# A linear-attention and gated-FFN kernel: the first batch in smaller pieces, with a new order of the whole program

## The chip, the core and the metric

The kernel runs on one core of a Trainium2 chip. The metric is the device time of one execution in microseconds (us); before the change the median of three runs is 379.01 us (378.92 to 380.15).

## What is computed

```python
def _attn_ref(q, k, v, w_phi):              # q, k, v: 8 batches, 8 heads, 576 tokens, 64
    def phi(x):
        proj = np.einsum('bhsd,df->bhsf', x, w_phi)              # 64 -> 128 features
        proj = proj - np.max(np.abs(proj), axis=-1, keepdims=True)
        return np.concatenate([np.exp(proj), np.exp(-proj)], axis=-1)
    q_p, k_p = (phi(q), phi(k))
    kv = np.einsum('bhsf,bhsd->bhfd', k_p, v)
    z = np.sum(k_p, axis=2)
    num = np.einsum('bhsf,bhfd->bhsd', q_p, kv)
    den = np.einsum('bhsf,bhf->bhs', q_p, z)[..., None] + 1e-06
    return num / den

def _moe_ref(x, w_gate, w_val, w_out):      # x: 4608 tokens, 512; 1536 inner columns
    gate = np.maximum(x @ w_gate, 0.0)
    val = x @ w_val
    return gate * val @ w_out
```

The attention's result of all heads is the FFN's x. Inputs and output are float32; the kernel multiplies in bf16.

## The kernel before, in words

**Tiling.** Each batch has 512 main tokens, in four chunks of 128, and a tail of 64; tails of two batches are worked together (`u`, `km`, `vm`, `qm`), and all tails make the FFN's ninth group. For batches 0 and 1 (`b < TURN`), keys are taken in pairs of heads, 36 blocks in all, cut by `K_CUTS` into five or six items per batch, and K and Q are transposed on TensorE; later batches use DMA transposes.

**Steps of a batch.** Each step is an *atom*: a small function with a key, made in the order of the code. For keys: `kT` transposes, `kTc` copies the transpose out of PSUM, `kr` multiplies by `w_phi` (64 rows of the array; two heads side by side on the two halves, `par` 0 and 1), `km` takes the maxima of the absolute values (DVE), `ke` the two exponentials (ACT), `kk` the scales, `vs` scales v by them (POOL, or DVE if the order's number has a prime), `kv` multiplies, `kvc` copies the result out. For queries: `qT`, `qTc`, `qc` (features by columns, for the exponentials `qe`), `qr` (features by rows, for the maxima `qm`), `qk` (the scale `cq`), `n` the numerators of three, three and two heads, `nt` and `nu` their sums on DVE, `xu` the division (a reciprocal on DVE, a product on POOL), then the transpose into x: `xT` and `xc` on TensorE for batches 0 and 1, `xd` by DMA after that.

**FFN.** Group g has 12 inner column blocks f: `fv` is the value half and `fg` the gate half (four matmuls each into a PSUM bank; the value half is copied to `val_sb` by ACT or DVE, the gate half is multiplied with it on DVE into `h`), `fo` the output matmuls in thirds, followed for the last third by a copy and the store. Group 0 is cut into steps by `FIRST`, entries of (first chunk, last chunk, first f, last f); the last tile of the ninth group is cut into columns by `LAST`.

**Order.** `ORDER`, a text of numbers, says in which order the atoms are written out; a prime chooses the other engine for a copy or a product; `z3` are three matmuls on zeros. Each engine runs its instructions in that order and waits on semaphores for what it reads and for buffers to come free. DMAs are issued by SP (loads in float32, transposes, stores), by ACT (halves of the last stores) and by POOL (loads that convert to bf16: q, k, the thirds of `wv` and `wg`, and `wo`); each issues them in its place among its other instructions. The first loads, of `w_phi`, k and v of batch 0, stand ahead of the order and are not changed. PSUM has eight banks, given out by `bank()`.

Of the kernel before, what the change touches and what calls it, by code (L numbers as in the profile page):

```python
# [8 lines left out]
FP32 = mybir.dt.float32  # L9
# [7 lines left out]

K_CUTS = [[4, 8, 16, 24, 32], [8, 16, 24, 32]]

FIRST = ((0, 2, 0, 4), (2, 4, 0, 4), (0, 4, 4, 12))  # L20
# [3 lines left out]


ORDER = """7 z3 82 92 93 83' 84 87 94 86 8 0 98 102 85 89 90 91 88 103 z1 104 96 97 108 105 95 107 106 z1 112
113 109 99 101 110' 111 122 114 115 123' 124 127 118 116 132 1 117 133 119 120 121 125 100' 128 z1
148 149 129 126 187 10 134 188 151 153 155 137 2 131 156 135 158 160 142 130 196 144 136 200 198
150 154 236 139 141 237 143 140 246 247 157 159 152 29 161 162 226 190 192 54 138 256 257 175 163
194 176 164 165 189 145 147' 191 266 177 146 3 267 193 4 169 170 166 167 171 168 195 199 181 178  # L30
182 321 214 5 172 179 183 180 184 201 197 217 215 11 220 221 218 222 219 208 9 322' 216 173 174'
282 283 223 209 185 186' 202 203 238 227' 210 205 206 204 207 240 211 1092 1093 1094 224 225' 239
1095 1096 324 328 228 229 242 212 213' 1097 326 232 1098 1099 1100 1101 1102' 231 6 1103 1104 1105
1106 1107 230 241 1108 243 268 269 270 271 273 258 274 272 261 248 251 260 249 253 255 254 1109 252
259 263 39 1110' 1111 1112' 264 1113 1114 275 250 233 1115 1116' 1117 290 361 262 363 265 292 365
279 280' 281' 323 327 291 295 293 1118 1119 294 1120' 1121 284 325 288 330 30 51 332 334 234 245
244 235 276 277 329 333 285 287 13 40 278' 289 1122 1123 351 296 1124 335 352 353 309 312 310 311
# [3 lines left out]
347' 32 55 61 371 372 307 308' 16 1134 63 388 398 402 399 391 400 383 385 1135' 1136 389 1137 401  # L41
42 403 1138' 405 393 367 368 369 395 392 394 390 1139 1140 1141 33 1142' 1143 1144' 17 43 424 426
428 384 418 454 458 420 1145 456 1146' 422 1147 1148 460 462 464 465 419 421 423 508 512 509 1149
# [4 lines left out]
502 1163 1164 1165' 534 536 538 564 529 531 523 1166 1167 568 503 570 476 574 566 533 569 571 1168  # L48
573 515 514 516 572 18 1169 1170 535 517 539 528 537 530 488 491 524 492 525 526 527 532 1171' 1172
1173 1174 1175 489 563 66 67 565 20 45 504 34 505 506 69 19 44 1176 1177 493 36 1178' 495 1179 567  # L50
507' 1180' 1181 494 490 590 555 496 497 1182' 593 575 591 68 587 588 589 540 1183 592 594 541 542
# [3 lines left out]
585 586 643 1199 1200 46 72 657 661 659 646 650 647 616 619 1201' 608 648 618 649 651 652 609 1202  # L55
# [3 lines left out]
675 676 716 717 741 1217 672 673 677 718 719 704 705 706 707 708 709 47 1218' 1219 1220 1221 1222  # L59
669 670 721 722 723 671 1223 1224 674 720 724 740 615 1225 1226 683 684 685 756 757 725 746 747 749  # L60
53 766 770 768 678 679 743 759 1227 1228 750 1229 1230' 710 711 712 760 713 758 761 763 714 680 681
# [4 lines left out]
1250' 1251 25 74 78 784 77 836 840 838 75 79 76 1252' 1253 831 832 1254 1255 1256' 1257 833 1258  # L66
814 846 847 848 1259 1260 785 786 828 829 830 787 48 834 835 815 817 818 1261 1262' 1263 800 1264
779 780 819 820 821 822 816 823 24 1265 37 1266 1267 1268 864 865 781 788 789 80 884 885 888 867
854 856 824 1269 1270' 866 1271 1272 887 858 889 868 855 857 849 1273 1274 891 850 851 869 859 900
904 902 874 877 28 894 896 1275 1276' 876 875 879 881 1277 1278 1279' 871 1280' 1281 843 878 886  # L70
880 898 844 845 852 1282 1283 81 895 899 901 903 929 933 1284 931 897 1285 905 1286 1287 964 870
853 930 934 968 890 965 935 937 966 1288' 1289 939 932 967 882 883 1290 872 873 974 978 976 861 936
# [4 lines left out]
1308 962 963 1309' 1310 1010 990 1008 1005 1040 1007 1012 57 1044 1006 1014 1009 991 1311 1042 1312  # L77
1313 1314 1051 1011 1000 1013 1045 1047 1049 1039 992 993' 1015 982 1315' 1043 1041 1316' 1001 1002
1003' 1317 1318' 1319 1320 1321 1322' 1323 1324' 971 972 1325 1016 973' 1023 983 1031 1055 1056
1326' 1024 1052 1327 1057 1025 1053 1054 1328' 1329 1034 1035 1330 1058 1059 1060 1061 1063 1064  # L80
1065 1331 1332 1333 1020 1036 1334' 1032 1033 1017 1018 1019 1021 1022 1062 1069 1335 1026 1027
1336 1337 1338 1028 1029 1030 1066 1067 1068 1339 1340 1070 1071 1037 1038 1074 1078 1075 1079 1072
1073 1077 1341 1342 1343 1344 1345' 1346 1347 1348' 1349 1350 1351' 1352' 1353 1354 1355 1356' 1357
1358' 1076 1080 1087 1359 1084 1085 1088 1089 1360 1361 1362 1363 1364' 1365 1366' 1367 1368' 1369
1086 1081 1082 1083 1090 1370 1371 1372 1091 1373 1374 1375 1376 1377 1378 1379 1380 1381' 1382
1383 1384' 1385 1386 1387' 1388 1389 1390' 1391 1392 1393 1394' 1395 1396 1397 1398' 1399 1400 1401
1402' 1403 1404' 1405 1406 1407 1408' 1409 1410' 1411 1412 1413 1414' 1415 1416 1417 1418 1419
1420' 1421 1422 1423 1424 1425 1426'"""
# [31 lines left out]
def kernel(  # L120
# [120 lines left out]
    def load_val_gate(t, w, i):  # L241
# [4 lines left out]
        )  # L246

    for i in range(NS):
        atoms.add("ld", f"wv{i}")(lambda alt, i=i: load_val_gate(wv_sb, moe_w_val, i))
        atoms.add("ld", f"wg{i}")(lambda alt, i=i: load_val_gate(wg_sb, moe_w_gate, i))  # L250
    atoms.add("ld", "wo")(
        lambda alt: nc.gpsimd.dma_start(
            out=wo_sb, in_=moe_w_out.rearrange("(c p) n -> p c n", p=P)
        )
    )
    for b in range(B):
        if b:
            atoms.add("ld", f"k{b}")(lambda alt, b=b: load_k(b))
# [23 lines left out]
    def turned_copy(st, n, by):  # L282
        st["T"] = sb_T.tile([P, n, P], BF16, name=f"tT{n}", bufs=3 if n == 4 else 2)
        copy_by(by)(st["T"].rearrange("p a b -> p (a b)"), st["pt"][:, 0 : n * P])

    for b in range(TURN, B):
        for n in "kq":

            @atoms.add("turn", n, b)
# [574 lines left out]
```

## Time and profile before

| | |
|---|---|
| median of three runs | 379.01 us (378.92 to 380.15) |
| profiled execution: its span | 377.4 us |
| median less that span, outside the program's instructions | 1.6 us |
| PE (TensorE) busy | 368.1 us, 98% |
| DVE (VectorE) busy | 290.7 us, 77% |
| ACT (ScalarE) busy | 213.1 us, 56% |
| POOL (GpSimd) busy | 151.3 us, 40% |
| moved by DMA | 45.10 MB, mean 120 GB/s |

The profile is of one execution; of its time only the span is given, from the first instruction of the program to the last. A share over the whole span hides stages: the rows by stage in the prediction are the ones to read. Matmuls overlap in the records, so a busy PE may still lose a little between two of them. An entry such as `L734` is a line of the kernel before; the functions above carry these numbers.

### The profile page before, as it was taken

The page shows a single profiled execution, that of the slowest core. Times are in us where ns is not written, and L with a number is a line of the kernel's source. Part 1 is how long each engine was busy: PE and PEld are TensorE (multiplying, and loading weights), DVE is VectorE, ACT ScalarE, POOL GpSimd, SP SyncE. Part 2 cuts the span into 40 slices and gives each one's busy share as a digit, 9 for nine tenths or more (in the row PEclk, how much of TensorE's full clock was granted, in tenths as well). Part 3 has the DMA queues.
Part 4 walks back from the last instruction along what each step waited for, and adds up shares of the span by engine and source line. Part 5 has one row for each costly group of instructions (what it writes and reads, how often), then busy time and mean ns, then how long its engine had stood idle before and what let it go on. Part 6 is the DMA issues. An engine that isn't in the chain of part 4 may idle for free.

```text
span 377.4 us, 8960 instructions
## 1 busy us (share of the span) xinstructions
PE 368.1 (98%) x3502; PEld 197.4 (52%) x3502; DVE 290.7 (77%) x633; ACT 213.1 (56%) x509; POOL 151.3 (40%) x201
## 2 busy tenths in 40 slices
PE   7789999999999999999999999999999999999996
PEld 4568465546545555464554554465455444444443
DVE  6998999988876799888868886988768927824641
ACT  6997888877687556876765359882740302111101
POOL 5883672488275275901842126933700210000000
PEclk9899999999999999999999999999999999999999
DMA  8999999999489959781289678620410130021004
GB/s 260 205 200 215 233 131 174 219 172 137 89 213 236 165 67 171 144 182 28 59 160 179 96 174 132 130 16 16 128 41 2 29 113 29 2 67 58 2 2 109
DMA packets 87929, 45.10 MB, mean 120 GB/s; under 512 B 55824, under 2 KB 82000, under 8 KB 87888
## 3 DMA queue, kind: packets, MB, share of 16 engines
q1 hardware_dynamic: 60208, 30.42, 37.3%
q0 software_dynamic: 27200, 13.57, 28.8%
q8 instruction: 27, 0.44, 0.5%
q10 hardware_dynamic: 480, 0.56, 0.5%
q14 instruction: 14, 0.11, 0.1%
HBM read 37.78 MB, written 9.44 MB: 125 GB/s over the span
## 4 chain that ended last, share of the span: by engine, by line
PE 92%; ACT 3%; DMA 3%; issue 0%; SPq 0%; DVE 0%; POOL 0%; DVEq 0%
PE pa L734 49%; PE pa L791 25%; PE pa L597 5%; PE pa L312 5%; PE pa L486 4%; PE pa L549 2%; DMA qn<-in_q_dram 2%; ACT qp L567 2%; PE pa L271 1%; PE pa L509 1%; DMA vn<-in_k_dram 1%; ACT kp L368 1%; ACT kv L422 0%; ACT val_sb L749 0%; ACT xT L662 0%
## 5 line engine op out<-in xcount | busy, mean ns | idle before, releaser
L791 PE MATMUL pa<-wo_sb,h 128*128 128x512 bf16 (+2 forms) x444 | 99.9, 373 | 0.0
L734 PE MATMUL pa<-xT,wv_sb 128*128 128x512 bf16 (+1 forms) x400 | 99.3, 370 | 0.1
L734 PE MATMUL pa<-xT,wg_sb 128*128 128x512 bf16 (+1 forms) x400 | 99.3, 370 | 0.0
L756 DVE SCALAR_TENSOR_TENSOR h<-pa,val_sb 128x512 bf16<-128x512 f32 (+1 forms) x112 | 74.6, 669 | 27.2 <-PE pa L734 20.5
L749 ACT CAST val_sb<-pa 128x512 bf16<-128x512 f32 (+1 forms) x67 | 38.1, 575 | 97.1 <-PE pa L734 88.0
L567 ACT ACTIVATE qp<-pa 128x512 bf16<-128x512 f32 x144 | 76.2, 618 | 15.1 <-PE pa L549 14.8
L368 ACT ACTIVATE kp<-pa 128x512 bf16<-128x512 f32 (+1 forms) x152 | 77.4, 605 | 11.1 <-PE pa L312 9.8
L328 POOL TENSOR_TENSOR vs<-vn,ek 128x512 bf16<-128x512 f32 (+1 forms) x68 | 67.4, 1005 | 31.1 <-DMA vn<-in_v_dram 15.2
L734 PEld LDWEIGHTS <-wv_sb 128*128 128x128 bf16 x448 | 41.9, 98 | 44.9 <-issue 1.2
L734 PEld LDWEIGHTS <-wg_sb 128*128 128x128 bf16 x448 | 41.6, 98 | 43.5 <-issue 0.7
L791 PEld LDWEIGHTS <-h 128*128 128x128 bf16 x444 | 40.8, 98 | 44.6 <-issue 0.8
L319 DVE TENSOR_REDUCE mq<-pa 128x4 f32<-128x512 f32 x72 | 46.5, 683 | 10.4 <-PE pa L312 10.1
L319 DVE TENSOR_REDUCE mk<-pa 128x4 f32<-128x512 f32 (+1 forms) x76 | 47.8, 653 | 3.9 <-ACT kp L368 2.3
L642 POOL TENSOR_TENSOR xu<-u,r 128x512 bf16<-128x512 f32 x22 | 22.8, 1041 | 67.4 <-DVE r L635 53.5
L642 POOL TENSOR_TENSOR tT<-u,r 128x512 bf16<-128x512 f32 x14 | 14.6, 1042 | 73.0 <-DVE r L635 41.0
L628 DVE TENSOR_TENSOR u<-pa,t 128x195 f32<-128x195 f32 (+3 forms) x120 | 38.2, 333 | 3.3
L616 DVE TENSOR_TENSOR t<-pa,cq 128x195 f32<-128x195 f32 (+3 forms) x120 | 36.8, 325 | 2.2 <-PE pa L597 1.0
L597 PEld LDWEIGHTS <-qp 128*128 128x128 bf16 x640 | 28.1, 98 | 14.0 <-ACT qp L567 0.9
L749 DVE CAST val_sb<-pa 128x512 bf16<-128x512 f32 (+1 forms) x45 | 30.7, 682 | 4.5 <-PE pa L734 3.0
L597 PE MATMUL pa<-kv,qp 128*128 128x65 bf16 x640 | 31.0, 193 | 0.9 <-ACT qp L567 0.5
L805 DVE COPY out_sb<-pa 128x512 f32<-128x512 f32 x13 | 8.9, 688 | 13.8 <-PE pa L791 13.6
L486 PEld LDWEIGHTS <-kp 128*128 128x128 bf16 x480 | 16.6, 98 | 3.9 <-issue 0.7
(71 smaller groups left out, 278.4 us busy)
## 6 DMA issues: line engine op xcount, KB each, us to landing
vn<-in_v_dram SPq DMA_DIRECT2D x6, 1024.0 KB, 7.3
qn<-in_q_dram POOLq DMA_DIRECT2D x8, 512.0 KB, 8.6
out_dram<-tT SPq DMA_DIRECT2D x16, 256.0 KB, 2.9
out_dram<-out_sb SPq DMA_DIRECT2D x16, 256.0 KB, 2.9
kn<-in_k_dram POOLq DMA_DIRECT2D x6, 512.0 KB, 9.1
wv_sb<-in_moe_w_val_dram POOLq DMA_DIRECT2D x3, 512.0 KB, 10.2
wg_sb<-in_moe_w_gate_dram POOLq DMA_DIRECT2D x3, 512.0 KB, 9.1
wo_sb<-in_moe_w_out_dram POOLq DMA_DIRECT2D x1, 1536.0 KB, 19.5
```

The lines of the kernel that those rows point to most:

```text
L319: nc.vector.tensor_reduce(m, some.rearrange("p (c f) -> p c f", f=F), axis=AX.X, op=ALU.max, apply_absolute_value=True,)
L328: eng.tensor_tensor(dst[:, :, s, 0:D], src, ek[:, :, s : s + 1].to_broadcast(list(src.shape)), op=ALU.mult,)
L368: nc.scalar.activation(st["kp"][:, s, 0 : n // 2, par, :], st["banks"][par][:, 0 : n // 2 * F].rearrange("p (a f) -> p a f", f=F), AF.Exp, ...
L567: nc.scalar.activation(x["qp"][:, s, slot].rearrange("p a b -> p (a b)"), st["cols", i][par], AF.Exp, scale=sign,)
L597: nc.tensor.matmul(pn[:, E * (2 * i + s) : E * (2 * i + s + 1)], lhsT=x["qp"][:, s, slot, blk, :], rhs=kv_of(b, lo + i)[:, s, :],)
L616: nc.vector.tensor_tensor(x["t", j][rows, 0:n], ab[:, :, 1], c[:, :, None].to_broadcast([np_, n, E]), op=ALU.mult,)
L628: nc.vector.tensor_tensor(x["u"][rows, lo : lo + n], ab[:, :, 0], x["t", j][rows, 0:n], op=ALU.add)
L642: copy_of(alt, nc.gpsimd, nc.vector).tensor_tensor(x["xu"], x["u"][:, :, 0:D], x["r"].to_broadcast([P, H, D]), op=ALU.mult)
L734: nc.tensor.matmul(ps, lhsT=w[:, dc, P * fi : P * fi + P], rhs=xTs[g][:, dc, lo:hi], start=(dc == 0), stop=(dc == NDC - 1),)
L749: copy_by(copy_of(alt, "ACT", "DVE"))(st["val", n], ps)
L756: nc.vector.scalar_tensor_tensor(st["h2"][:, fi, lo:hi], ps, 0.0, st["val", n], op0=ALU.max, op1=ALU.mult)
L791: nc.tensor.matmul(po, lhsT=st["h2"][:, fi, P * t : P * t + P], rhs=wo_sb[:, fi, c0:c1], start=(fi == 0), stop=(fi == NFC - 1),)
```

## The change

For batch 0 four things are cut smaller, one load is cut in three, and the order is another one throughout. `SPLIT` names both Q items of batch 0: their `qc` and `qr` become atoms of one half (`par`) each, which is one token chunk, and `qk` one per chunk. `FIRST` gives group 0's first steps one chunk of 128 tokens for blocks 0 to 3; a step now always fills a PSUM bank, with up to four blocks f side by side (`nf`), and its eviction is always 512 wide. `KV_LAST` takes the last four of a half's 18 blocks of k and v into a second piece of `kv`. `wo` is loaded in three thirds. Which of two buffers takes `xu` and the output tile follows from the chunk's number and no more from a count over the order. Options that are there but unused (`PLAIN` is empty, `Q_TURN` and `X_TURN` are equal to `TURN`) are left out below.

```diff
-FIRST = ((0, 2, 0, 4), (2, 4, 0, 4), (0, 4, 4, 12))
+FIRST = ((0, 1, 0, 4), (1, 2, 0, 4), (0, 2, 4, 8), (2, 4, 0, 8), (0, 4, 8, 12))
...
+SPLIT = {(0, 0), (0, 1)}
+KV_LAST = {0: 4}
...
-ORDER = """7 z3 82 92 93 83' 84 87 94 86 8 0 98 102 85 89 90 91 88 103 z1 104 96 97 108 105 95 107 106 z1 112
+ORDER = """z3 84 94 85 95 86 87 89 104 96 90 88 9 100 105 10 91 98 z1 106 2 99 97 101 124 110 107 109 125 114
...
-    atoms.add("ld", "wo")(
-        lambda alt: nc.gpsimd.dma_start(
-            out=wo_sb, in_=moe_w_out.rearrange("(c p) n -> p c n", p=P)
+    def load_wo(i):
+        part = slice(4 * i, 4 * (i + 1))
+        nc.gpsimd.dma_start(
+            out=wo_sb[:, part], in_=moe_w_out.rearrange("(c p) n -> p c n", p=P)[:, part]
         )
-    )
+
+    for i in range(NFC // 4):
+        atoms.add("ld", f"wo{i}")(lambda alt, i=i: load_wo(i))
...
+        last = [x for x in order if x[2] >= 2 * CP * (part + 1) - KV_LAST.get(b, 0)]
+        order = [x for x in order if x not in last] + last
+        cuts = [0, len(order) - len(last), len(order)]
+        for piece, (lo, hi) in enumerate(zip(cuts, cuts[1:])):
...
+            @atoms.add("kv", b, part, piece)
...
-            @atoms.add("qc", *key, i)
-            def _(alt, i=i):
-                st["cols", i] = [bank(), bank()]
-                for par in range(2):
...
+            for pars in ((0,), (1,)) if split else ((0, 1),):
+                at = (i, *pars) if split else (i,)
+
+                @atoms.add("qc", *key, *at)
+                def _(alt, i=i, pars=pars):
+                    for par in pars:
+                        st["cols", i, par] = bank()
...
+                @atoms.add("qr", *key, *at)
...
+        for ci in range(len(chunks) if split else 1):
+
+            @atoms.add("qk", *key, *((ci,) if split else ()))
...
+                step = slice(ci, None, 2) if split else slice(0, None)
+                nc.scalar.activation(st["c"][:, step], st["m"][:, step], AF.Exp, scale=2.0)
...
-                if by_dma and x_count[0] % 2:
+                if by_dma and spare:
...
-            steps = [(fi, P * lo, P * hi) for lo, hi, f0, f1 in FIRST for fi in range(f0, f1)]
+            steps = [
+                (fi, C // (hi - lo), P * lo, P * hi)
+                for lo, hi, f0, f1 in FIRST
+                for fi in range(f0, f1, C // (hi - lo))
+            ]
...
+        def half_step(fi, nf, w, lo, hi):
+            ps = bank().rearrange("p (f n) -> p f n", f=nf)
+            for i in range(nf):
+                for dc in range(NDC):
+                    nc.tensor.matmul(
+                        ps[:, i],
+                        lhsT=w[:, dc, P * (fi + i) : P * (fi + i + 1)],
+                        rhs=xTs[g][:, dc, lo:hi],
...
-                st["val", n] = sb_g.tile([P, SF], BF16, name="val_sb")[:, 0 : hi - lo]
+                st["val", n] = sb_g.tile([P, SF], BF16, name="val_sb")
...
-        def out_tile():
-            if t_count[0] % 2:
+        def out_tile(t):
+            if (4 * g + t) % 2:
```

What the new order moves is seen engine by engine. First SP's queue at the program's start: ahead of these rows stand only the first pieces of k and v, which are the same in both. Before:

```order
L220 DMA vn_105<-in_k_dram 128x2x576
L220 DMA vn_109<-in_v_dram 128x576
L220 DMA vn_109<-in_v_dram 128x2x576
L298 DMA_TRANSPOSE qmT<-qm 128x4x128
L220 DMA vn_740<-in_v_dram 128x4x576
L292 DMA_TRANSPOSE kT_1047<-kn 128x16x128
```

Now:

```order
L236 DMA vn_105<-in_k_dram 128x2x576
L236 DMA vn_109<-in_v_dram 128x576
L236 DMA vn_109<-in_v_dram 128x2x576
L252 DMA vm<-in_v_dram 64x8x64 x2
L236 DMA vn_766<-in_v_dram 128x4x576
L319 DMA_TRANSPOSE qmT<-qm 128x4x128
```

The v tails of unit 1 (`vm`) follow batch 0's loads at once, and v of batch 1 (`vn_766`) no longer stands behind the transpose of the q tails. On POOL, not shown here, the load of the first third of `wv` moves from ahead of batch 0's first `vs` to behind its last, with the first two thirds of `wg` behind it.

Second, DVE around the FFN's first evictions: `t` and `u` are the sums of the numerators, `r` the reciprocal that ends a chunk, `h` the product of gate and value half. Before, the rows up to the first product:

```order
L616 TENSOR_TENSOR t<-pa,cq 128x195
L628 TENSOR_TENSOR u<-pa,t 128x130
L628 TENSOR_TENSOR u<-pa,t 128x195 x2
L284 COPY tT_761<-pa 128x1024
L635 RECIPROCAL r<-u 128x8
L616 TENSOR_TENSOR t<-pa,cq 128x130
L616 TENSOR_TENSOR t<-pa,cq 128x195
L628 TENSOR_TENSOR u<-pa,t 128x130
L616 TENSOR_TENSOR t<-pa,cq 128x195
L628 TENSOR_TENSOR u<-pa,t 128x195 x2
L635 RECIPROCAL r<-u 128x8
L756 SCALAR_TENSOR_TENSOR h_823<-pa,val_sb 128x256
```

Now, the rows up to the first value half's copy; just ahead of them stands the reciprocal of chunk 1:

```order
L686 TENSOR_TENSOR t<-pa,cq 128x195
L698 TENSOR_TENSOR u<-pa,t 128x130
L698 TENSOR_TENSOR u<-pa,t 128x195
L303 COPY tT_739<-pa 128x512
L731 COPY xT<-pa 128x4x128
L686 TENSOR_TENSOR t<-pa,cq 128x195
L731 COPY xT<-pa 128x4x128
L686 TENSOR_TENSOR t<-pa,cq 128x195
L698 TENSOR_TENSOR u<-pa,t 128x195
L686 TENSOR_TENSOR t<-pa,cq 128x195
L705 RECIPROCAL r<-u 128x8
L821 CAST val_sb<-pa 128x512
```

Before, the copies of x (`xT`) were on ACT and all four reciprocals stood ahead of the first product; now DVE copies chunks 0 and 1 of x itself, and the FFN's first eviction stands behind the third reciprocal.

Third, the end of the program on DVE; `COPY` takes an output tile out of PSUM ahead of its store. Before:

```order
L749 CAST val_sb<-pa 128x512
L756 SCALAR_TENSOR_TENSOR h_6191<-pa,val_sb 128x512
L805 COPY tT_6354<-pa 128x512
L805 COPY tT_6388<-pa 128x512
L805 COPY u<-pa 128x160
```

Now:

```order
L830 SCALAR_TENSOR_TENSOR h_6273<-pa,val_sb 128x512 x2
L881 COPY tT_6448<-pa 128x512
L881 COPY tT_6456<-pa 128x512
L881 COPY out_sb<-pa 128x512
L881 COPY out_sb<-pa 128x352
```

The 160-column piece of the last tile was the last one out; now the 352-column piece is, and it is copied by DVE.

More of the change, by code (lines that the diff above doesn't have):

```diff
@@ L284, in turned_copy @@
         copy_by(by)(st["T"].rearrange("p a b -> p (a b)"), st["pt"][:, 0 : n * P])
-    for b in range(TURN, B):
-        for n in "kq":
+    for b in range(min(TURN, Q_TURN), B):
+        for n, first in (("k", TURN), ("q", Q_TURN)):
+            if b < first:
+                continue
             @atoms.add("turn", n, b)
@@ L351, in _ @@
                 st["T"] = T()
-            st["banks"] = [bank(), bank()]
+            st["banks"] = {par: bank() for par in range(2)}
             rows_of(st["T"], st["banks"])
@@ L361, in _ @@
                 row_max(st["m"][:, par:n:2], st["banks"][par][:, 0 : n // 2 * F])
+                if plain:
+                    if "nm" not in st:
+                        st["nm"] = sb_s.tile([P, 8, 2], FP32, name="ek")
+                    nc.vector.tensor_scalar(
+                        st["nm"][:, par:n:2, 0], st["m"][:, par:n:2], -1.0, None, op0=ALU.mult
+                    )
             @atoms.add("ke", *key, par)
@@ L720 @@
             q_tails(b // 2)
[L723 removed]
     def ffn(g):
         st = {}
[L727 removed]
+        steps = [(fi, 1, 0, SF) for fi in range(NFC)]
         if g == 0:
[L729 to L749 removed]
+            steps = [
+                (fi, C // (hi - lo), P * lo, P * hi)
+                for lo, hi, f0, f1 in FIRST
+                for fi in range(f0, f1, C // (hi - lo))
+            ]
@@ L751, in _ @@
+        for n, (fi, nf, lo, hi) in enumerate(steps):
+            @atoms.add("fv", g, n)
+            def _(alt, n=n, fi=fi, nf=nf, lo=lo, hi=hi):
+                ps = half_step(fi, nf, wv_sb, lo, hi)
+                st["val", n] = sb_g.tile([P, SF], BF16, name="val_sb")
+                copy_by(copy_of(alt, "ACT", "DVE"))(
+                    st["val", n], ps.rearrange("p f n -> p (f n)")
+                )
             @atoms.add("fg", g, n)
-            def _(alt, n=n, fi=fi, lo=lo, hi=hi):
+            def _(alt, n=n, fi=fi, nf=nf, lo=lo, hi=hi):
@@ L769, in store @@
+        def out_tile(t):
+            if (4 * g + t) % 2:
+                return sb_g.tile([P, DM], FP32, name="out_sb", bufs=2)
+            t = sb_T.tile([P, 8, P], BF16, name="tT8", bufs=2)
+            return t.rearrange("p a b -> p (a b)").bitcast(FP32)
         def store(t, out_sb, c0, c1):
```

226 lines of the change are left out of this document (117 added, 109 removed), and 47 rows, old and new, of the table ORDER.

## The prediction

> **What bounds the kernel now.** First the page: the span, and how much of it each engine works.
>
> ```profile
> span 377.4 us, 8960 instructions
> PE 368.1 (98%) x3502; PEld 197.4 (52%) x3502; DVE 290.7 (77%) x633; ACT 213.1 (56%) x509; POOL 151.3 (40%) x201
> ```
>
> TensorE (PE) is the bound, but an average hides where it is not. So the second view is the busy time by stage. I cut at the first Q transpose (12.6), the first FFN matmul (28.9), the point after which nothing waits (35), and the last output matmuls (363.2). Columns: stretch, its length, busy time and count of PE, weight loads, VectorE (DVE), ScalarE (ACT), GpSimd (POOL), granted clock, DMA share, GB/s.
>
> ```profile
> 0.00:12.60 12.60, 8.94 (x57) 4.68 (x57) 8.92 (x17) 9.30 (x27) 7.35 (x19) 1.00 0.96 246
> 12.60:28.90 16.30, 14.54 (x318) 10.99 (x319) 16.00 (x46) 15.39 (x41) 14.67 (x21) 0.90 1.33 203
> 28.90:35.00 6.10, 5.94 (x72) 4.89 (x69) 4.98 (x13) 5.75 (x14) 2.70 (x3) 1.00 1.27 186
> 35.00:363.20 328.20, 328.20 (x3005) 171.39 (x3004) 258.38 (x556) 181.63 (x428) 126.54 (x160) 1.00 0.63 111
> 363.20:377.40 14.20, 10.53 (x61) 5.46 (x59) 2.40 (x5) 1.04 (x2) 0.00 (x0) 1.00 0.28 74
> ```
>
> From 35 us on PE is busy without a break: every stall a new order makes there adds its whole length, and none is there to be removed. From 12.6 to 28.9 DVE works 16.00 of 16.30 us and ACT 15.39; this start, before the FFN can feed PE, is the only place to win. Third view, the chain that ended last, in the first 35 us (start, length, what):
>
> ```profile
> 3.79 8.76 DMA qn<-in_q_dram
> ...
> 12.60 1.78 PE pa L271 x16
> ...
> 15.81 2.05 ACT qp L567 x4
> ...
> 25.62 0.98 ACT qp L567 x2
> ...
> 28.73 0.35 PE pa L597 x6
> 29.07 1.31 PE pa L734 x12
> ...
> 342.62 20.72 PE pa L734 x96
> ```
>
> The chain goes from the landing of Q's first load (12.55) through the transposes, the exponentials on ACT (15.81 to 26.60) and the rest of chunks 0 and 1 to the FFN. (The last row is from the same view of the whole span: a 512-column matmul takes 20.72/96 = 0.216 us; the row above it: 256 columns take 0.109.)
>
> So the end is: the time of the first FFN matmul, plus the PE work left then, plus stalls after it, plus the tail. The change can act on these four only.
>
> **Term 1, the first FFN matmul.** The new order keeps nearly all of batch 0's attention ahead of it: the transposes of chunks 0 and 1 both stand before it, and so do all numerator groups but one. Its time is the latest of three paths.
>
> *ACT.* From the first Q exponential to the last:
>
> ```profile
> 15.80 2.06 ACT L567 ACTIVATE qp<-pa 128x512 bf16<-128x512 f32 x4 [0.41 <-PE pa L549]
> ...
> 23.09 0.38 ACT L422 CAST kv<-pa 128x260 bf16<-128x260 f32 x1
> ...
> 25.40 0.22 ACT L583 ACTIVATE cq<-mq 128x16 f32<-128x16 f32 x1
> ...
> 25.51 1.08 ACT L567 ACTIVATE qp<-pa 128x512 bf16<-128x512 f32 x2
> ...
> 28.75 0.58 ACT L284 COPY tT<-pa 128x512 bf16<-128x512 bf16 x1
> ```
>
> That is 25.51 + 1.08 - 15.80 = 10.8 us. The new order loses one kv copy there (-0.3, about what it takes until the next instruction starts) and gains one small exponential (+0.1) and two 512-wide copies (+1.0): 11.6. The first may start about 0.1 later, so ACT ends at 27.5, or at 26.7 if it is packed as tightly as the row of four, 0.5 each, by which I put 0.8 of the 10.8 down as idle. Behind it stand numerators and the transpose of chunk 1 (0.7 from rows like 28.73): 27.4 to 28.2.
>
> *DVE.* From the copies of Q's transposes to the reciprocal that ends chunk 1:
>
> ```profile
> 13.99 1.28 DVE L284 COPY tT<-pa 128x1024 bf16<-128x1024 bf16 x2
> ...
> 21.30 0.42 DVE L284 COPY tT<-pa 128x512 bf16<-128x512 bf16 x1
> ...
> 23.16 0.42 DVE L422 CAST kv<-pa 128x260 bf16<-128x260 f32 x1
> ...
> 24.90 0.28 DVE L616 TENSOR_TENSOR t<-pa,cq 128x130 f32<-128x130 f32 x1
> ...
> 26.02 0.20 DVE L635 RECIPROCAL r<-u 128x8 f32<-128x8 f32 x1
> ```
>
> 26.02 + 0.20 - 13.99 = 12.2 us. The new order takes three 512-wide copies away (-1.2) and adds a kv copy and one product (+0.6): 11.6. The start moves, though: SP now issues the v tails of unit 1 (2 x 128 KB) right behind the first loads, beside Q's. Bounds: 0 if Q has the engines first, and their bytes at the rate of stretch one if it shares: 0.26 MB / 246 GB/s = 1.1 us. I take 0.8, near the upper end, because stretch two shows DMA loaded (1.33). The Trainium skill, "DMA: Bandwidth & Descriptors", section "Queues, rings and completion order", says that each DMA engine takes packets from its queues in turn, so Q would share. By it the upper end would hold and the sum would be the same, since the weights are later still; no run here shows it yet. With 0 to 1.1 the reciprocal ends between 25.6 and 26.7. Behind it come the division on POOL (1.0), the transpose (0.3) and 0.3 of latency: 27.2 to 28.3.
>
> *The weights.* The first FFN matmul needs the first third of wv. Before, POOL issued it ahead of its first vs; now it stands behind all of POOL's vs work of batch 0.
>
> ```profile
> 16.23 0.76 POOL L243 DMA_DIRECT2D wv_sb<-in_moe_w_val_dram  x1
> ...
> 18.14 1.05 POOL L328 TENSOR_TENSOR vs<-vn,ek 128x512 bf16<-128x512 f32 x1
> ...
> 20.68 0.62 POOL L328 TENSOR_TENSOR vs<-vn,ek 128x256 bf16<-128x256 f32 x1
> ...
> 25.38 2.04 POOL L642 TENSOR_TENSOR xu<-u,r 128x512 bf16<-128x512 f32 x2 [0.44 <-DVE r L635]
> ...
> DMA to landing us min/median/max: 10.1/10.2/12.3
> ...
> DMA to landing us min/median/max: 4.3/7.3/11.7
> ```
>
> (The last two rows are the landings of wv and of Q, from the view by tile.) POOL's last vs ends at 21.3. It takes over two from DVE (+1.05 +0.62) and sheds two issues of weights (-0.76 each): the issue comes at 21.4. It can land 4.3 us later (Q's shortest) or 10.2 (wv's median): 25.7 to 31.6. By bytes: 12.6 is when Q landed; ahead of wv's landing now lie the K of batch 1 (0.59 MB, part of it moved), another third of wv, Q of batch 1 and this third (0.52 each) at the 203 GB/s of stretch two, 10.7 us less about 1 already moved, and the v tails and V of batch 1 (1.44 MB in all; V stood behind a wait for the q tails before) at between 203 and the best rate of any 5 us shown below, 340: 4.2 to 7.1. So 26.5 to 29.4, the middle 28.0. As it comes with spread at just the time of the other paths, the latest of the three is later than each: I take **28.5**, against 28.91: **-0.4**. Ends: 27.2 and 30.
>
> **Term 2, the PE work left.** Behind the start now stand 8 half-row matmuls of batch 1's K and 4 of a numerator, and FFN pieces are narrower.
>
> ```profile
> 26.97 0.61 PE L271 MATMUL pa<-ident,qn 128*128 128x128 bf16 x8
> ...
> 31.61 0.62 PE L312 MATMUL pa<-w,tT 64*128 64x128 bf16 x16
> ```
>
> Half of the 16 is 0.21 (the last one's 0.2 lies over the next); the four are 4/6 of 0.35 less overlap, 0.12. A 128-column matmul takes (0.61 - 0.22)/7 = 0.056, half of a 256-column one and no less: 64 of them for 32 cost +0.07, and 64 of 256 for 32 of 512 cost +0.06. The sum is **+0.45**. Splitting Q into single halves makes PE stream them one by one where two ran side by side, but ahead of the start, where PE sat idle; it costs nothing while ACT and DVE are the cover, at most some 1 us if they weren't. The kv split has the same matmuls, on PE's idle time too. FFN evictions fall from 16 pairs to 12, which DVE has no need of after 35.
>
> **Term 3, stalls after it.** Before, the row from 28.9 to 35 shows 0.16 idle; records of matmuls overlap, so that up to 0.5 may be lost in it. After, the first two gate thirds land behind wv, at 0.52 MB / 203 GB/s = 2.6 us each. The first gate piece comes some 3.4 us after the first matmul (three value pieces of 0.87, four numerators, 0.7 of batch 1), the one of the second third at about 6.3, against 2.6 and 5.2: just in time. POOL's last gate third waits for the landing of wv's first, and the divisions of chunks 2 and 3 queue behind that wait on POOL; they are needed some 5 us after the first FFN matmul, so the wait costs nothing if wv let that matmul start. **0** (-0.5 to +1). The three wo loads move the same bytes as one and are used only after the FFN pieces of batch 0; cost 0 while these cover them, and what they land late if not.
>
> **Term 4, the tail.**
>
> ```profile
> 371.15 0.69 DVE L805 COPY tT<-pa 128x512 f32<-128x512 f32 x1 [4.49 <-PE pa L791]
> ...
> 372.94 0.45 ACT L805 COPY out_sb<-pa 128x352 f32<-128x352 f32 x1 [3.79 <-PE pa L791]
> ...
> 373.84 0.32 DVE L805 COPY u<-pa 128x160 f32<-128x160 f32 x1 [2.00 <-PE pa L791]
> ...
> out_dram<-out_sb ACTq DMA_DIRECT2D x1, 88.0 KB, 2.4
> ...
> out_dram<-u ACTq DMA_DIRECT2D x1, 40.0 KB, 2.1
> ```
>
> The last piece was 160 columns; it now is 352, and on DVE. Between 160 (0.32) and 512 (0.69) that copy takes 0.52: +0.2. Its store lands in 2.4 instead of 2.1: +0.3. **+0.5**, with nothing behind to hide it.
>
> **Sum.** -0.4 + 0.45 + 0 + 0.5 = +0.55 on the profiled span of 377.4. What lies around the span (379.01 median - 377.4 = 1.6) stays: **379.5 us**. A measurement of this kernel can tell about 0.3%, 1.1 us, so this is no change that could be told.
>
> **Rivals.**
>
> *Faster.* ACT's idle goes, Q isn't delayed, wv lands in time, the 0.5 of stalls goes too: -1.7 (27.2) + 0.45 + 0.5 - 0.5 = -1.25, 377.8. For it: three paths whose lower ends agree near 27.2. Against: three must hold at once. Chance 0.15.
>
> *Slower, by the weights.* The third of wv lands 8.5 us after its issue (29.9), inside its rows' 4.3 to 10.2, and the gate thirds follow late: first FFN at 30.0, +1.1 + 0.45 + 0.5 = +2.05, 381.1. It decides from a landing past 29.1, 7.7 us behind the issue. For it: POOL's loads landed 10.1 to 12.3 after issue here. Against: a short queue at that time. Chance 0.25.
>
> *Slower, by the clock.* The stretches of 5 us show it falling:
>
> ```profile
> 5.00:10.00 5.00, 4.36 (x26) 2.83 (x22) 3.73 (x8) 4.46 (x17) 2.74 (x5) 1.00 1.11 340
> 10.00:15.00 5.00, 3.76 (x45) 2.65 (x47) 4.87 (x10) 4.94 (x18) 4.49 (x7) 0.77 1.30 204
> 15.00:20.00 5.00, 4.22 (x112) 2.93 (x106) 4.77 (x10) 4.59 (x14) 4.21 (x8) 0.88 1.25 206
> ```
>
> At half speed that is 0.23 and 0.12 of 5 us doubled: 2.3 + 1.2 = 3.5 us at 12.7 to 16.1. PE waits longer for a later Q, so a second such stretch, or one by a new stall after the start, can come. It costs at most its half, 1.7 us, where PE is the bound, and a little where it isn't; with the 0.55 it gives 379.6 to 381.3, say 380.8. The Trainium skill, "TensorE: Matmul & The Clock Gate", section "What's actually happening", has the clock set by activity in windows of 3.4 us, which agrees with the 3.5 worked out here. A stall of the same size anywhere from 35 to 363 has the same price. Chance 0.18 for both.
>
> The forecast itself has 0.42, with a range of its own from 378.0 to 380.1. So: faster 0.15, same 0.42, slower 0.43. Range: from the fast rival, 377.8, to the weights', widened to 381.3.
>
> **What would show it.** Right: the first FFN matmul between 28 and 29, no PE idle after 36, the last store's landing 0.5 later behind the last matmul. Wrong: PE idle ahead of that matmul put down to wv, a granted clock under 1 in two stretches, or a start before 27.5. Any PE stall over 0.5 us after 36 us would break term 3.

## The result, and the profile after

Median after: 418.44 us (412.11 to 419.86, four runs) against 379.58 us (378.92 to 381.06) before on the same chip; the ratio is 1.0925, interval 1.0845 to 1.1005. The forecast was 379.5 us. The ratio is taken over the runs within 1.5% of the fastest of their kernel, here 417.26 and 412.11 us; the profiled execution, 419.63 us, is 1.8% above the fastest, and its parts are read against its own span.

First the page of the changed kernel: the span, the busy time, PE by slice and the granted clock by slice.

```profile
span 417.9 us, 9017 instructions
...
PE 380.3 (91%) x3516; PEld 205.7 (49%) x3566; DVE 294.4 (70%) x642; ACT 219.0 (52%) x526; POOL 138.2 (33%) x181
...
PE   7799986999988999999977999999989989996995
...
PEclk9969999899999999999996999999999999998999
```

The span is 40.5 us longer. PE's idle time went from 9.3 (377.4 - 368.1) to 37.6 us (417.9 - 380.3), +28.3. Some 2.6 us of that are no idle time: 50 matmuls are missing from the records (3516 of them against 3566 weight loads), and each leaves a gap of about 0.05 us. The busy time rose by 12.2, though the work hardly changed. In part these are slower matmuls; in part they are matmuls cut off by a wait, which show their whole 0.38 us where the next would start after 0.22. Both idle time and clock show in the slices: the 7s, 8s and 6s come in the middle too, and the clock falls in several places.

The same by stage, columns as in the prediction, cut at the first Q transpose (14.30), the first FFN matmul (33.33), 40 and 400 us of the kernel after:

```profile
0.00:14.30 14.30, 10.20 (x56) 5.08 (x56) 9.16 (x18) 7.60 (x22) 8.48 (x20) 1.00 0.98 233
14.30:33.33 19.03, 16.61 (x308) 12.76 (x308) 14.77 (x40) 15.91 (x42) 11.83 (x18) 0.82 1.13 212
33.33:40.00 6.67, 6.05 (x99) 5.42 (x99) 5.19 (x15) 5.14 (x10) 6.12 (x8) 1.00 1.45 161
40.00:400.00 360.00, 333.90 (x2986) 175.81 (x3034) 259.91 (x564) 189.52 (x452) 111.77 (x137) 0.98 0.60 99
400.00:417.90 17.90, 13.57 (x72) 6.61 (x70) 5.37 (x8) 0.88 (x2) 0.00 (x0) 1.00 0.21 60
```

The start is 4.4 us later (33.33 against 28.91), and the long stretch, without any idle time before, has 26.1 us of it (some 23.6 without the 48 records that are missing there). What PE waits for (columns: total in us, times, longest; L806 are the FFN's two halves, L867 the output matmuls):

```profile
PE pa L806 <- issue: 9.8, 3, 4.7
PE pa L867 <- DMA wo_sb<-in_moe_w_out_dram: 3.7, 1, 3.7
PE pa L806 <- DVE mk L340: 3.3, 4, 1.4
```

"issue" hides DMAs here: the longest of these matmuls starts 0.09 us after an x transpose has landed. Three waits stand out.

**The last third of wo**, in the timeline (start, length):

```profile
56.22 4.52 SPq L313 DMA_TRANSPOSE kT<-kn  x1
...
56.55 0.81 POOL L269 DMA_DIRECT2D wo_sb<-in_moe_w_out_dram  x1
...
72.75 1.32 PE L867 MATMUL pa<-wo_sb,h 128*128 128x512 bf16 x4 [3.66 <-DMA wo_sb<-in_moe_w_out_dram]
```

POOL issues it at 56.55, 0.33 us behind SP's transposes of k (56.22). It lands at 72.71, and PE has waited 3.66 us for it; the transposes land at 72.51.

**x of group 4:**

```profile
213.80 0.94 POOL L230 DMA_DIRECT2D kn<-in_k_dram  x1
...
214.25 1.22 SPq L719 DMA_TRANSPOSE xT<-xu  x1
...
215.57 6.48 SPq L313 DMA_TRANSPOSE qT<-qn  x1
...
222.30 2.29 PE L806 MATMUL pa<-xT,wv_sb 128*128 128x512 bf16 x5 [4.69 <-issue]
```

The x transpose is issued 0.45 us behind a load of k and lands when that has nearly landed, at 222.21, 8.0 us after its issue; undisturbed ones take 2.4.

**The mixed x of the tails:**

```profile
369.67 1.04 POOL L711 TENSOR_TENSOR xu<-u,r 128x512 bf16<-128x512 f32 x1 [35.44 <-DVE r L705]
374.05 0.59 ACT L881 COPY out_sb<-pa 128x512 f32<-128x512 f32 x1 [14.09 <-PE pa L867]
374.66 1.20 SPq L848 DMA_DIRECT2D out_dram<-out_sb  x2
...
375.94 2.54 SPq L719 DMA_TRANSPOSE xT_mix<-xu  x2
...
379.81 1.18 PE L806 MATMUL pa<-xT_mix,wv_sb 128*128 128x512 bf16 x4 [4.07 <-issue]
```

Its input is ready at 370.7, but in SP's queue two output stores stand ahead that wait for ACT's copies; SP comes to it 5.2 us later. Before, the last of these transposes was issued 11.4 us ahead of its reader:

```profile
331.09 1.19 SPq L650 DMA_TRANSPOSE xT_mix<-tT  x1
...
342.46 1.03 PE L734 MATMUL pa<-xT_mix,wv_sb 128*128 128x512 bf16 x4
```

Each of the three waits brings a stretch at half clock (the column of 0.51), which begins behind it or, at x of group 4, within it:

```profile
220.00:227.00 7.00, 4.70 (x12) 1.66 (x13) 1.38 (x2) 0.29 (x2) 0.00 (x0) 0.51 1.51 196
73.30:76.80 3.50, 3.50 (x23) 1.86 (x22) 1.29 (x5) 1.35 (x3) 0.67 (x1) 0.51 0.54 48
380.50:384.00 3.50, 3.50 (x10) 1.26 (x9) 0.00 (x0) 1.17 (x2) 0.00 (x0) 0.51 0.02 5
```

Half of PE's busy time there is lost, (4.70 + 3.50 + 3.50)/2 = 5.9 us. With the waits, 3.7 + 4.7 + 4.1, the three cost 18.3 us.

### The profile page after: what moved, and what is told of

It reads as the page before. It is cut to its first block, busy times and chain, and to the rows that moved or that the text cites. A ratio compares the mean times of both kernels' runs of the same rounds, so it can differ in the third digit from the quotient of the medians.

```text
span 417.9 us, 9017 instructions
## 1 busy us (share of the span) xinstructions
PE 380.3 (91%) x3516; PEld 205.7 (49%) x3566; DVE 294.4 (70%) x642; ACT 219.0 (52%) x526; POOL 138.2 (33%) x181
## 4 chain that ended last, share of the span: by engine, by line
PE 66%; DVE 12%; ACT 8%; DMA 7%; issue 4%; POOL 2%; SPq 0%; POOLq 0%; DVEq 0%; ACTq 0%
PE pa L806 39%; PE pa L867 15%; ACT kp L407 4%; PE pa L667 4%; DMA wo_sb<-in_moe_w_out_dram 4%; DVE mk L340 4%; DVE mq L340 3%; PE pa L333 3%; PE pa L540 3%; DMA xT<-xu 2%; ACT qp L633 2%; POOL vs L349 2%; PE pa L614 2%; DVE h L830 1%; PE pa L290 1%
## 5 line engine op out<-in xcount | busy, mean ns | idle before, releaser
L867 PE MATMUL pa<-wo_sb,h 128*128 128x512 bf16 (+2 forms) x428 | 102.2, 379 | 5.3 <-DMA wo_sb<-in_moe_w_out_dram 3.7
L806 PE MATMUL pa<-xT,wv_sb 128*128 128x512 bf16 (+2 forms) x417 | 95.1, 361 | 8.9 <-issue 5.7
L806 PE MATMUL pa<-xT,wg_sb 128*128 128x512 bf16 (+2 forms) x415 | 93.1, 354 | 3.1 <-DVE mk L340 2.0
L830 DVE SCALAR_TENSOR_TENSOR h<-pa,val_sb 128x512 bf16<-128x512 f32 x108 | 73.9, 688 | 28.9 <-PE pa L806 25.5
L821 ACT CAST val_sb<-pa 128x512 bf16<-128x512 f32 x64 | 37.7, 594 | 80.3 <-PE pa L806 72.2
L349 POOL TENSOR_TENSOR vs<-vn,ek 128x512 bf16<-128x512 f32 (+1 forms) x58 | 58.1, 1012 | 45.9 <-ACT ek L421 42.4
L806 PEld LDWEIGHTS <-wv_sb 128*128 128x128 bf16 x480 | 44.3, 99 | 58.8 <-issue 19.0
L867 PEld LDWEIGHTS <-h 128*128 128x128 bf16 x444 | 40.9, 98 | 48.8 <-issue 6.9
L806 PEld LDWEIGHTS <-wg_sb 128*128 128x128 bf16 x480 | 43.2, 97 | 43.8 <-issue 3.9
L821 DVE CAST val_sb<-pa 128x512 bf16<-128x512 f32 x44 | 30.1, 688 | 37.1 <-PE pa L806 30.5
L667 PE MATMUL pa<-kv,qp 128*128 128x65 bf16 x640 | 33.4, 195 | 2.3 <-DVE mk L340 1.2
L711 POOL TENSOR_TENSOR tT<-u,r 128x512 bf16<-128x512 f32 x10 | 10.4, 1042 | 47.4 <-DVE r L705 47.4
L881 ACT COPY out_sb<-pa 128x512 f32<-128x512 f32 x11 | 6.4, 585 | 35.7 <-PE pa L867 33.0
L540 PEld LDWEIGHTS <-kp 128*128 128x128 bf16 x480 | 16.3, 98 | 4.9 <-issue 1.5
```

Of the source, the lines that this page charges most:

```text
L349: eng.tensor_tensor(dst[:, :, s, 0:D], src, ek[:, :, s : s + 1].to_broadcast(list(src.shape)), op=ALU.mult,)
L667: nc.tensor.matmul(pn[:, E * (2 * i + s) : E * (2 * i + s + 1)], lhsT=x["qp"][:, s, slot, blk, :], rhs=kv_of(b, lo + i)[:, s, :],)
L711: copy_of(alt, nc.gpsimd, nc.vector).tensor_tensor(x["xu"], x["u"][:, :, 0:D], x["r"].to_broadcast([P, H, D]), op=ALU.mult)
L806: nc.tensor.matmul(ps[:, i], lhsT=w[:, dc, P * (fi + i) : P * (fi + i + 1)], rhs=xTs[g][:, dc, lo:hi], start=(dc == 0), stop=(dc == NDC - 1),)
L821: copy_by(copy_of(alt, "ACT", "DVE"))(st["val", n], ps.rearrange("p f n -> p (f n)"))
L830: nc.vector.scalar_tensor_tensor(st["h2"][:, fi : fi + nf, lo:hi], ps, 0.0, st["val", n].rearrange("p (f n) -> p f n", f=nf), op0=ALU.max, ...
```

## The experiments

Three theories: the new order of the body costs (1); the smaller pieces cost (2); the late start costs and drags the rest along (3). All kernels are the changed code with another text in `ORDER`, shown by the atoms' keys. Runs of different sets are compared by their ratios to the kernel before, which ran beside each.

**The old order on the new code.**

```diff
-ORDER = the new order
+ORDER = the order of before; pieces of one old atom one behind the other
```

> The changed code with the order of before written onto its atoms: Q halves, kv pieces and the three wo loads one right behind the other, group 0's 128-token steps where the 256-token steps of the same blocks stood. Theory 1 (the new order costs, the smaller pieces do not): 379.5 to 381, first FFN matmul at about 29, no PE wait over 1 us after 36. Theory 2 (the smaller pieces and the buffers chosen by the chunk's number cost): over 390. Theory 3 (the late start costs and drags the rest along): as theory 1, since the start is the old one.

Measured 380.50 us, ratio 1.0011 (0.9982 to 1.004), first FFN matmul at 29.04, and all that PE waits for after 36 us is this row:

```profile
PE pa L867 <- issue: 0.3, 2, 0.2
```

Theory 2 falls: split Q, 128-token steps, two kv pieces and three wo loads cost nothing that can be measured. The order is the cause. Its text also chooses engines: 114 steps, 46 copies of value halves and 14 scalings of v among them, are on another engine in the new order, and no run separates these choices from the places.

**Half of each order.**

```diff
 first run: new order to ("fo", 0, 0, 0, 0)
+then what is left, in the order of before
 second run: order of before to ("fo", 0, 0, 0, 0)
+then what is left, in the new order
```

> The new order up to the first output matmul of group 0 (about 56 us), then what is left in the order of before. Theory 1 (order of the body): the start's 4.4 us and little more, 383 to 387. Theory 2 (smaller pieces): no forecast of its own beyond what the run with the old order gives. Theory 3 (the late start drags the rest along): over 395.

> The order of before up to the first output matmul of group 0, then what is left in the new order. Theory 1 (order of the body): the start's 4.4 us come back and nothing else, about 414, with PE waiting again at the landings of wo, x and the mixed x of the tails. Theory 3 (the late start drags the rest along): 380 to 390.

New start: 392.97 us, ratio 1.0321 (1.0231 to 1.041), more than theory 1 said; in the traced execution PE waited 5.3 us for the third wo load. New body: 405.95, ratio 1.0665 (1.0608 to 1.0722), with the waits at x (4.53) and the mixed x (4.06) back. Theory 3 falls: with the old start the body still loses 6.7%.

**Three waits mended.**

```diff
 ("ld", "wo0")
+("ld", "wo1") ("ld", "wo2")
 ("xd", 4, 3)
+("ld", "k6")
 ("xu", "u", 3, 0)
+("xd", 8, 3) ("xd", 8, 1)
```

> The new order with five DMA issues moved and no other instruction: the second and third wo load right behind the first; the load of k of batch 6 ahead of the last two x transposes of batch 4 by about 14 us; the last two mixed x transposes ahead of two output stores in SP's queue. Theory 1 in its narrow form (three late landings carry the loss): 3.7 + 4.7 + 4.1 us of PE waits go and about 4.5 us of half clock with them: about 401. Rival (the waits only move: PE, DVE and the buffers of the new order are short everywhere): over 411.

398.29 us, ratio 1.051 (1.046 to 1.056): about 16 us less by the ratios, 20 by the medians, against 17 expected. Five DMA issues moved, and no other instruction; PE's busy time falls by 8.0 us and the long waits are gone. The transposes of k, issued at 58.21 without wo beside them, land in 4.98 us and no longer in 16.3. Not all of the gain is the moves': of the 21.7 us between the two traces, 2.7 lie ahead of the first FFN matmul (30.59 against 33.33), where nothing was moved.

```profile
PE 372.3 (94%) x3516; PEld 202.8 (51%) x3566; DVE 294.0 (74%) x642; ACT 218.5 (55%) x526; POOL 138.2 (35%) x181
...
PE pa L806 <- DVE mk L340: 3.3, 4, 1.4
PE pa L333 <- DVE tT L303: 1.4, 1, 1.4
PE pa L667 <- DVE mk L340: 1.2, 2, 0.8
```

**The same by halves.** The two moves of the body on the kernel with the old start, and the wo loads on the one with the new start.

```diff
 old start, new body
+("ld", "k6") and the two ("xd", 8, ...) moved as above
 new start, old body
+("ld", "wo1") ("ld", "wo2") behind ("ld", "wo0")
```

> The order of before up to the first output matmul of group 0, then the new order with the load of k of batch 6 and the last two mixed x transposes moved as in the run with three waits mended. If the losses add up by place: 406.0 less 4.5 and 4.1 us of waits and some 3 us of half clock, 393 to 395. If the waits only move on: over 399.

> The new order up to the first output matmul of group 0, then the order of before, with the second and third wo load right behind the first. If the wo loads made the 5.3 us wait and what follows it: 384 to 386, which leaves the start's 4 to 5 us over the order of before. If the start drags more along: over 389.

394.25 us, ratio 1.0342 (1.0261 to 1.0423), and 386.20 us, ratio 1.0131 (1.0052 to 1.021): the first as expected where losses add up by place, the second 0.2 above it. So the start costs some 5 us (2 to 8 by the interval), and 13 us (10 to 16) are left in the body.

**The start.**

```diff
 ("kk", 0, 2)
+("ld", "q1") ("ld", "wv0")
...
 ("ld", "v1")
+("ld", "vm1")
```

> The run with three waits mended, and at the start the q load of batch 1 and the first-needed third of wv are issued on POOL some 10 us earlier, where it waits for the scales, and the v tails of unit 1 behind v of batch 1. If POOL's late issue of wv sets the start: wv lands by 26, the first FFN matmul comes at 28.5 to 29.5 and the whole is 1 to 2 us faster than that run, 396 to 397.5. Rival (batch 0's attention sets it, or wv's early bytes delay k and q): first FFN matmul at 30 or later, the same time or slower.

403.07 us, ratio 1.0573 (1.0503 to 1.0643), first FFN matmul at 36.38: the rival was right. The two issues stand ahead of POOL's scaling of v, and kv now waits for that:

```profile
16.01 0.95 POOL L230 DMA_DIRECT2D qn<-in_q_dram  x1 [5.24 <-PE pa L333]
...
16.95 0.76 POOL L259 DMA_DIRECT2D wv_sb<-in_moe_w_val_dram  x1
...
18.41 0.30 PE L572 MATMUL pa<-vs,kp 64*128 64x65 bf16 x8 [1.14 <-POOL vs L349]
...
20.11 0.41 PE L572 MATMUL pa<-vs,kp 64*128 64x65 bf16 x8 [1.40 <-POOL vs L349]
```

Issued 7 us earlier, wv landed at 28.92, only 1.6 us earlier than in the kernel with three waits mended (issue 23.94, landing 30.54). This trace also has half the clock from 18.7 to 32.3 us, which the other one doesn't; how much of the 36.38 that is stays open.

**What is left in the body, first idea: banks freed too late.** 103, then 222 steps of DVE and ACT moved nearer to the matmuls whose banks they read.

```diff
 each ("km", ...), ("qm", ...), ("nu", ...)
+at most 3, 2, 4 matmul steps behind its matmuls (103 moved)
 second run: also ("ke", ...), ("qe", ...), ("kvc", ...)
+no farther behind than in the order of before (222 moved)
```

> As the run before it in this list, and 103 DVE steps behind group 0's first output matmul are moved nearer to the matmuls whose PSUM bank they read: maxima of k to at most 3 and of q to at most 2 matmul steps behind theirs, the second sum of a numerator to at most 4 where its first sum allows. Theory (in the new order the banks come free too late: on average the last reader stands 6.1 matmul steps behind a numerator against 3.1 in the order of before, 3.2 against 0.8 for the maxima of q): 3 to 8 us faster than the run without it, PE's waits for DVE gone. Rival (the small waits come from DVE's and POOL's load, not from the distances): within 1.5 us of it, or slower, as DVE then waits in its queue for PE.

> The kernel with the start of before and two moves mended, PE's order kept, and 222 steps of DVE and ACT behind group 0's first output matmul moved as near to the matmuls that they read as in the order of before or nearer (maxima and exponentials of k and q, second sums of the numerators, copies of kv). Theory (the steps that free PSUM banks stand too far behind): 4 to 9 us less, 385 to 390. Rival (it is PE's own order: work written ahead of what it needs, x, kv and the scaled v): within 1.5 us of 394, or slower, since DVE and ACT then wait in their queues for PE.

396.19 us, ratio 1.0385 (1.0314 to 1.0455), no gain on 1.0342; and 402.06, ratio 1.0579 (1.0502 to 1.0656), 9 us worse. The idea falls as far as mending goes.

**Second idea: x too late for its reader.** Counted in the two orders, matmuls by their measured lengths, the PE work between the last x transpose of groups 2 to 8 and its first reader (the lead of x) is 6.6, 10.8, 13.4, 11.1, 10.1, 9.6 and 13.1 us before, and 2.9, 7.4, 3.7, 6.8, 1.6, 2.6 and 0.9 now. First mended in the new order, then made short in the old one, last the first together with the 222 steps.

```diff
 new body: ("fv"/"fg", 2 and 7, ...)
+some 2.5 us of PE work later; ("ld", "k7") ("ld", "q7") ahead of ("xd", 5, 1)
 order of before: the last ("xd", g, ...) of g = 2 to 8
+later, to the new order's distance from its reader
```

> The kernel with the start of before and two moves mended, and three places more: the first FFN blocks of groups 2 and 7 are written some 2.5 us of PE work later, behind work of the group before, so that 5 us and more of PE work lie between the last x transpose and its first reader (2.9 and 2.6 in the new order); k and q of batch 7 are loaded ahead of the last two x transposes of batch 5. Theory (too little PE work between an x transpose and its reader): 2 to 3.5 us faster than the kernel without it. Rival (the waits only move on): within 1 us of it.

> The converse: the order of before on the changed code, and nothing moved but the last x transpose of groups 2 to 8, seven instructions of SP, later, so that as much PE work is left between it and its first reader as in the new order (2.9, 6.9, 3.7, 7.4, 1.6, 2.6, 0.9 us where the order of before has 6.6, 10.8, 13.4, 11.1, 10.1, 9.6, 13.1). Theory: a transpose lands 2.4 us after its issue alone, and 4 to 8 beside a load, so PE waits at groups 6 and 8 at least, 2.5 to 6.5 us in all: 383 to 387. Rival (the lead of x does not matter): 380 to 381.

> The same with the later first FFN blocks of groups 2 and 7 and the earlier loads of k and q of batch 7. Theory (banks and x together make the waits that are left): 3 us less again, 383 to 387. Rival (each mended wait only moves on while PE's order stays): 392 to 396.

Mending: 396.45 us, ratio 1.0419 (1.0379 to 1.0459), no gain on 1.0342, and with the 222 steps 406.42, ratio 1.0702 (1.062 to 1.0785): the waits moved on. In the first trace PE waits for no x at all any more; what the waits at x were worth, 2.8 us in the kernel it started from, came back elsewhere. The converse: 391.71 us, ratio 1.0297 (1.0259 to 1.0334). Seven SP instructions moved, and 11 us lost, where 2.5 to 6.5 were expected. Group 2 in its timeline:

```profile
112.50 0.95 POOL L230 DMA_DIRECT2D kn<-in_k_dram  x1
...
112.80 1.36 SPq L719 DMA_TRANSPOSE xT<-xu  x1
...
121.36 1.87 PE L806 MATMUL pa<-xT,wv_sb 128*128 128x512 bf16 x4 [5.49 <-issue]
...
121.40:125.00 3.60, 3.60 (x9) 1.24 (x10) 0.00 (x0) 0.59 (x1) 0.00 (x0) 0.50 1.51 204
```

The transpose again shares the DMAs with a load of k, and here with one of v, issued at 112.28, and takes 8.5 us; then 3.6 us at half clock, half of them lost. With the other waits at x, 1.3, 1.1 and 0.5 (groups 7, 8 and 3), that is 10.2 us.

**Third idea: two readers of one bank.** DVE's maximum (`mk`) and ACT's exponentials (`kp`) read the same PSUM bank. Paired by the order of their atoms, they overlap in none of 76 pairs of any run so compared, and the second often starts some 30 ns behind the end of the first: 15 pairs before, 34 after. The waits for each other, before (L319, L368) and after:

```profile
DVE mk L319 <- ACT kp L368: 2.3, 5, 1.1
ACT kp L368 <- DVE mk L319: 1.2, 2, 0.6
```

```profile
DVE mk L340 <- ACT kp L407: 13.8, 15, 2.2
ACT kp L407 <- DVE mk L340: 18.9, 13, 3.4
```

Put close together in the old order:

```diff
 in 24 places, ("km", ...) some five matmul steps ahead of ("ke", ...)
+right ahead of it
```

> The order of before on the changed code; in 24 places DVE's maximum of a k bank is written right ahead of ACT's exponentials of the same bank and no longer some five matmul steps ahead. Theory (the two readers of a bank run one after the other, and where they are written close together one engine waits in its queue for the other): more pairs that follow each other at once, ACT waiting for DVE some 5 to 15 us, and 1 to 4 us of it on PE: 382 to 384. Rival (such waits stay on engines that have the time): 380 to 381.

386.84 us, ratio 1.0176 (1.014 to 1.0211): 6 us lost, more than expected, 28 pairs at once behind each other, and:

```profile
ACT kp L407 <- DVE mk L340: 12.0, 13, 2.0
```

The Trainium skill, "PSUM — Partial Sum Buffer", section "PSUM bank collisions raise a hardware error", says that the compiler's scheduler keeps two engines apart wherever they touch one bank and the same 32 partitions, reads as well as writes. The 76 pairs agree.

**Attention or FFN?** One order on each kind of step.

```diff
 first run: attention's steps as in the new order (two moves mended)
+FFN's steps, and the places between, as before
 second run: attention's steps and the places as before
+FFN's steps among themselves as in the new order
```

> The changed code with the order of before up to the first output matmul of group 0; behind it the attention's steps (with the two moves mended) follow one another as in the new order, the FFN's as in the order of before, and the places at which FFN steps stand between attention steps are those of the order of before. Theory (the 13 us that are left come from the order within the attention): 390 to 395. Rival (they come from where the FFN's steps stand between the attention's): 380.5 to 384.

> The counterpart: attention's steps and the places for FFN steps of the order of before, the FFN's steps among themselves in the new order. Theory (order within the attention): 380.5 to 383, with one wait at group 5, whose first step now stands 1.7 us of PE work behind its last x transpose. Rival (order within the FFN): over 386.

433.27 us, ratio 1.1404 (1.1333 to 1.1475), and 399.32, ratio 1.0504 (1.0427 to 1.058). The first is far outside both of its forecasts; the second is over the 386 of its rival. No single kind of step is the culprit by these runs: both mixtures are worse than the order of before (1.0011) and than the new body with its two moves (1.0342). In the first no wait is over 1.9 us, there are only more of them. The second's largest wait is the one foreseen at group 5, of 3.9 us; the rest is small ones:

```profile
PE pa L806 <- DMA xT<-xu: 3.9, 1, 3.9
```

**One thing that the smaller pieces allow.**

```diff
 ("xc", 0, 0)
+("fv", 0, 0)
 ("xT", 0, 1)
```

> The order of before on the changed code, and group 0's first FFN step, four blocks on the first 128 tokens, ahead of the transpose of the second chunk of x: the one thing that the smaller first piece allows. If PE's idle time ahead of the FFN can be used: first FFN matmul at 28 and 0.3 to 0.5 us less than the order of before. Rival (the work moved only takes the place of other work): the same within 0.3 us.

380.63 us, ratio 1.0016 (0.9995 to 1.0037): the same; the first FFN matmul came at 28.73 instead of 29.04, waiting for the copy of x. No version beat the kernel before.

## Why the prediction was wrong

**"Every stall a new order makes there adds its whole length"** was the right reading of before, and the reason why it failed: the next step, **Term 3, put those stalls at 0 (-0.5 to +1)**. It looked at the weights of the first steps and at nothing behind 40 us, while the order changed throughout. The trace has some 24 us of idle time there and some 6 of half clock, of which the three waits are 18.3. Its sentence on wo, "what they land late if not", named the price (3.7 us, as measured) but gave it no chance. What could have been read ahead of any run is the count of the second idea: the PE work between an x transpose and its reader fell from 6.6 to 13.4 us to as little as 0.9, while the trace of before had such transposes landing up to 6.8 us after their issue beside a load. By those numbers groups 6 and 8 should stall, and 2, 4 and 7 wherever a load lies beside. PE did wait for x in groups 2, 4, 5, 7 and 8 (0.95, 4.69, 0.84, 1.05 and 4.07 us), but not in group 6: the count tells where a wait threatens, and neither that it comes nor how long it is.

**The clock rival** had the mechanism and one such stall in mind, at most 1.7 us. There were three with 5.9. The Trainium skill, "TensorE: Matmul & The Clock Gate", section "What's actually happening", has the gate work in windows of 3.4 us; the stretches here, 3.4 and 6.8 us, agree.

**Term 1** said 28.5, and 33.33 came. POOL issued wv's first third at 24.44 and not at 21.4: it stood 3.60 us waiting for scales of k, and the load of q (0.95) stood among its scalings of v.

```profile
17.92 2.06 POOL L349 TENSOR_TENSOR vs<-vn,ek 128x512 bf16<-128x512 f32 x2 [3.60 <-ACT ek L421]
...
21.05 0.95 POOL L230 DMA_DIRECT2D qn<-in_q_dram  x1
...
24.44 0.82 POOL L259 DMA_DIRECT2D wv_sb<-in_moe_w_val_dram  x1
...
33.33 1.05 PE L806 MATMUL pa<-xT,wv_sb 128*128 128x128 bf16 x16
```

The landing 5.8 us later (30.27) was in the range; the issue was mis-sized by 3 us. So the weights came when their rival had them (29.9), but by a late issue, where the rival had a late landing. From 30.27 to 33.33 it was no longer the weights. That rest goes with 6.8 us at half clock (22.1 to 29.0): the kernel with three waits mended, the same up to there, started the FFN at 30.59 without them, 0.05 us behind its landing of wv. Q's delay by the v tails was taken at 0.8 and bounded by 1.1; with the tails behind it Q landed at 12.98, with them ahead at 14.46, its issue within 0.1 us: 1.5, more than the bound. So Q shares, as the Trainium skill says ("DMA: Bandwidth & Descriptors", "Queues, rings and completion order").

**Term 2**, +0.45, fits the old order on the new code: 1.0011 is +0.4 us, its interval -0.7 to +1.5.

**Term 4**, +0.5, was right. The last matmuls in the chains of before and after:

```profile
363.34 10.40 PE pa L791 x60
```

```profile
407.08 6.56 PE pa L867 x36
```

From their end to the span's end it took 3.66 us before and 4.26 after, +0.6.

**What stays open.** Late landings cost 16 to 20 us and the start about 5. Of the 13 us left, runs showed that x's short leads alone (11 us) and close bank readers alone (6) can cost that much in the old order. Longer leads in the new one brought nothing, since the trace without a wait at x had others in their place. No run moved the new order's bank readers apart: the new body with its two moves has 27 pairs that follow each other at once, and the runs of the first idea still 24 and 21. That either is the cause of the 13 us is therefore not shown.

## What to carry to other kernels

Where the bound engine never waits, judge a new order by its leads: for each transfer, count the bound engine's work between issue and first reader, and compare it with the slowest landing of that kind in the trace, not the median. Look also at what stands ahead of an issue in its queue, above all stores that wait for a copy. What helped here were single issues moved where a trace showed PE waiting for them. Steps moved by a rule, even towards their inputs, brought nothing (103 of them) or cost 9 us (222).

## What the runs showed of the hardware

A DMA transpose of x that lands in 2.4 us alone took 8.0 and 8.5 beside a load of k and what else was moving, and those of k, which land in 4.65 to 5.86 us elsewhere in that trace, took 16.3 beside wo. The issue of the transposes of Q held SP for 6.48 us beside that load of k.

The granted clock can miss a slow stretch. The same 64-row matmuls in the kernel with the new start and early wo loads, then in the one with three waits mended; the row of the first's clock says 1.00 at that time:

```profile
25.57 2.46 PE L572 MATMUL pa<-vs,kp 64*128 64x65 bf16 x70
...
20.00:28.00 8.00, 8.00 (x153) 6.17 (x148) 4.78 (x11) 5.52 (x17) 6.18 (x10) 1.00 1.19 208
```

```profile
23.53 1.25 PE L572 MATMUL pa<-vs,kp 64*128 64x65 bf16 x72
```

70 took twice as long as 72: the durations, not the clock's column, tell the rate. The first FFN matmul came at 33.75 in the one and 30.59 in the other.
